# Centring x in place of W1, weights loaded behind the first heads, and attention in thirds of the sequence: a change to a fused attention and MLP kernel on one Trainium2 core

## The chip, the cores and the metric

The kernel runs on one core of one Trainium2 chip. Five engines work side by side, each with its own queue that runs in order: TensorE (PE; its weight loads are shown as PEld), VectorE (DVE), ScalarE (ACT), GpSimd (POOL) and SyncE (SP, which here only issues DMAs). Inputs lie in HBM; data is worked on in SBUF, and matmuls write to PSUM. The metric is device time in microseconds. Three runs of the kernel before took 345.12, 343.38 and 345.32 us (median 345.12).

## The reference

Four batches, 8 heads, 768 positions, head size 64. Each query sees only the 6 chunks (of 32 keys) with the largest upper bound of its score; the result goes through a layer norm and a two-layer MLP.

```python
k_min, k_max = k_chunks.min(3), k_chunks.max(3)          # 24 chunks of 32 keys
ub = sum(maximum(q * k_min, q * k_max), -1)              # bound of each query on each chunk
ub = where(causal, ub, -1e9); top = argsort(ub)[..., -6:]
scores = where(in_top_chunk & (i >= j), q @ k.T / 8, -1e9)
x = softmax(scores) @ v                                   # heads side by side: (4, 768, 512)
xn = (x - mean(x)) / sqrt(var(x) + 1e-6) * g_ln
out = x + maximum(xn @ w_ch1, 0) @ w_ch2                  # 512 -> 2048 -> 512
```

## The kernel before

**Units of work.** A "head" below is a pair of heads `g` of one batch (16 pairs, four to a batch), for two heads fill the 128 partitions (64 values each). A sequence is six blocks of 128 positions. For each `g` the kernel runs these pieces:

- `load_qk` (L183): two DMAs for q and two for k, issued by SP. `load_v` (L193): two DMAs with a cast, issued by POOL, and a memset.
- `prep_q` (L201): six transposes on PE into the PSUM tile `tr`, one ACT copy (`qh`), then on DVE `ql` (L211), `rh` (L214), `rl` (L215) and the copies into `QA` and `QB` (L218, L219).
- `prep_k` (L222): six transposes into `tr`, DVE minimum and maximum over the chunks (L230, L231), two ACT copies (`KA`, `KB`), and small DVE steps that fill `BD`.
- `bounds` (L243, 20 matmuls), `select` (L257, DVE: two additions, ten MAX8, one comparison), `mask_t` (L274, five transposes and two DVE copies). The mask enters the scores as extra rows of `QA` and `QB`.
- `score_bin` (L287): for each head of the pair six bins of scores in PSUM tiles `mm`, each followed by one ACT Exp into `pt`; `diag` (L310, DVE): multiplies the six diagonal blocks by a triangle `Lmask`; `values` (L317): 21 matmuls per head; `normalise` (L331, DVE), once per head of the pair.
- `x_t` (L341): six transposes and one DVE copy give one row of `xT`.

For each batch there are `stats` (L355, DVE, bn_stats over 512 values for each block), `mlp1` (L376, 32 pieces: four matmuls and one ACT Relu each) and `mlp2` (L391, 24 pieces of four matmuls; after each fourth one DVE step `ot` and one output DMA on SP).

**Weights.** POOL loads and casts W1 and W2 in four DMAs each (L147, L152). W1 is multiplied by `g_ln` (`w1_scale`, L155, DVE), its mean over the input features is formed (`w1_mean`, L160, 16 matmuls and four ACT copies) and taken off (`w1_center`, L168, DVE), so that x itself need not be centred.

**Order.** Every piece is given a time by `at(t, fn)` (L410 to L450), where one unit is a head: head `g` has its scores at `g`, its preparation up to two units ahead. The MLP of batch `b` starts at `4(b+1)+0.25`, beside the heads of batch `b+1`; the last MLP has nothing beside it. The pieces are written in order of these times (L453). The framework then orders the instructions by priority and by a model of when their inputs are ready, so an instruction can come ahead of its written place; on the chip each queue runs in the order so fixed.

**Buffers.** `tr` has one buffer of two PSUM banks, `mm` three of one bank, `sm` two, `trh` one. q and k have three buffers, v four.

Of the kernel before, what the change touches and what calls it, by code (L numbers as in the profile page):

```python
# [9 lines left out]
ACTF = mybir.ActivationFunctionType  # L10
# [8 lines left out]
def kernel(  # L19
# [12 lines left out]

    nc = tc.nc
# [6 lines left out]
    NT = S // P  # L40
    HP = H // 2
# [13 lines left out]
    SB0 = S - P  # L55
# [3 lines left out]
    ldp = ctx.enter_context(tc.tile_pool(name="ldp", bufs=3))  # L59
    vap = ctx.enter_context(tc.tile_pool(name="vap", bufs=4))  # L60
    prp = ctx.enter_context(tc.tile_pool(name="prp", bufs=2))
    smp = ctx.enter_context(tc.tile_pool(name="smp", bufs=2))
    ptp = ctx.enter_context(tc.tile_pool(name="ptp", bufs=3))
    xp = ctx.enter_context(tc.tile_pool(name="xp", bufs=2))
    htp = ctx.enter_context(tc.tile_pool(name="htp", bufs=1))
    outp = ctx.enter_context(tc.tile_pool(name="outp", bufs=3))

    PSUM = bass.MemoryType.PSUM
    ps_t = ctx.enter_context(tc.tile_pool(name="ps_t", bufs=1, space=PSUM))
# [4 lines left out]
    q_r = q.rearrange("b h (t p) d -> b p t h d", p=P)  # L74
    k_r = k.rearrange("b h (t p) d -> b p t h d", p=P)
    v_r = v.rearrange("b h (t p) d -> b p t h d", p=P)
    out_r = out.rearrange("b (t p) n -> b t p n", p=P)

    pieces = []

    def at(t, fn):
        pieces.append((t, len(pieces), fn))
# [4 lines left out]
    Lmask = const.tile([P, P], F16, name="Lmask", tag="Lmask")  # L87
    causb = const.tile([P, NT - 1, NCH], F32, name="causb", tag="causb")
    RT = const.tile([P, S], F16, name="RT", tag="RT")
    mean_w = const.tile([P, P], F16, name="mean_w", tag="mean_w")  # L90
    mhalf = const.tile([P, NT], F32, name="mhalf", tag="mhalf")
    NR = 3
    QA = [ring.tile([P, S], F16, name=f"QA{i}", tag=f"QA{i}") for i in range(NR)]
    QB = [ring.tile([P, S], F16, name=f"QB{i}", tag=f"QB{i}") for i in range(NR)]
    KA = [ring.tile([P, S], F16, name=f"KA{i}", tag=f"KA{i}") for i in range(NR)]
    KB = [ring.tile([P, S], F16, name=f"KB{i}", tag=f"KB{i}") for i in range(NR)]

    BD = [ring.tile([P, 2, 2, 2, NCH], F16, name=f"BD{i}", tag=f"BD{i}") for i in range(2)]
    MN = [ring.tile([P, NT - 1, P], F16, name=f"MN{i}", tag=f"MN{i}") for i in range(2)]

    def consts_first():
        make_identity(nc, ident_f)
        nc.vector.tensor_copy(ident_h, ident_f)
        for i in range(2):
            nc.vector.memset(BD[i], 0.0)
        for i in range(2):
            nc.vector.memset(MN[i], 0.0)
        nc.gpsimd.memset(causb, 0.0)
        nc.gpsimd.affine_select(
            out=causb, in_=causb, compare_op=ALU.is_ge, fill=CAUSAL,  # L110
            base=P, pattern=[[P, NT - 1], [-CH, NCH]], channel_multiplier=1,
        )
        nc.gpsimd.memset(RT, 0.0)
        for r0 in (0, 64):
            rr = RT[r0:r0 + NCH, :]
            nc.gpsimd.memset(rr, -NEGM)
            nc.gpsimd.affine_select(
                out=rr, in_=rr, compare_op=ALU.is_ge, fill=0.0,
                base=0, pattern=[[1, S]], channel_multiplier=-CH,
            )  # L120
            nc.gpsimd.affine_select(
                out=rr, in_=rr, compare_op=ALU.is_ge, fill=0.0,
                base=CH - 1, pattern=[[-1, S]], channel_multiplier=CH,
            )
        nc.gpsimd.memset(Lmask, 1.0)
        nc.gpsimd.affine_select(
            out=Lmask, in_=Lmask, compare_op=ALU.is_ge, fill=0.0,
            base=0, pattern=[[1, P]], channel_multiplier=-1,
        )
        nc.gpsimd.memset(mhalf, -0.5)  # L130
        nc.gpsimd.memset(mean_w, 1.0 / DM)

    def consts_ring(i):
        nc.vector.tensor_copy(KA[i][64:P, :], RT[64:P, :])
        nc.vector.tensor_copy(KB[i][0:64, :], RT[0:64, :])
        nc.vector.memset(QA[i][64:P, 0:P], 0.0)
        nc.vector.memset(QB[i][0:64, 0:P], 0.0)
# [5 lines left out]
    w1mean = const.tile([P, HID], F16, name="w1mean", tag="w1mean")  # L143
    w1_r = moe_w_ch1.rearrange("(kt p) n -> p kt n", p=P)
    w2_r = moe_w_ch2.rearrange("(kt p) n -> p kt n", p=P)

    def w1_load(kt):  # L147
        if kt == 0:
            nc.sync.dma_start(gstr, moe_g_ln.rearrange("(kt p) -> p kt", p=P))
        nc.gpsimd.dma_start(w1b[:, kt, :], w1_r[:, kt, :])  # L150
# [3 lines left out]

    def w1_scale(kt):  # L155
        nc.vector.tensor_scalar(
            w1b[:, kt, :], w1b[:, kt, :], gstr[:, kt:kt + 1], None, op0=ALU.mult,
        )

    def w1_mean(j):  # L160
        mp = ps_m.tile([P, 512], F32, name="mm", tag="mm")
        for kt in range(KT1):
            nc.tensor.matmul(
                mp, mean_w, w1b[:, kt, 512 * j:512 * j + 512], start=(kt == 0), stop=(kt == KT1 - 1),
            )
        nc.scalar.copy(w1mean[:, 512 * j:512 * j + 512], mp)

    def w1_center(kt):  # L168
        nc.vector.tensor_tensor(w1b[:, kt, :], w1b[:, kt, :], w1mean, ALU.subtract)  # L169
# [13 lines left out]
    def load_qk(g):  # L183
        b, hp = divmod(g, HP)
        qn = ldp.tile([P, NT, 2, D], F32, name="qn", tag="qn")
        kn = ldp.tile([P, NT, 2, D], F32, name="kn", tag="kn")
        for hh in range(2):
            nc.sync.dma_start(qn[:, :, hh, :], q_r[b, :, :, 2 * hp + hh])
        for hh in range(2):
            nc.sync.dma_start(kn[:, :, hh, :], k_r[b, :, :, 2 * hp + hh])  # L190
        st[g].update(qn=qn, kn=kn)

    def load_v(g):  # L193
        b, hp = divmod(g, HP)
        va = vap.tile([P, 2, NT, 80], F16, name="va", tag="va")
        for hh in range(2):
            nc.gpsimd.dma_start(va[:, hh, :, 0:D], v_r[b, :, :, 2 * hp + hh])  # L197
        nc.gpsimd.memset(va[:, :, :, D:D + 1], 1.0)
        st[g].update(va=va)

    def prep_q(g):  # L201
        qn = st[g]["qn"]
        pst = ps_t.tile([P, S], F32, name="tr", tag="tr")
        for t in range(NT):
            nc.tensor.transpose(pst[:, t * P:(t + 1) * P], qn[:, t, :, :], ident_f)  # L205
        qh = prp.tile([P, S], F16, name="qh", tag="qh")
        ql = prp.tile([P, SB0], F16, name="ql", tag="ql")
        rh = prp.tile([P, SB0], F16, name="rh", tag="rh")
        rl = prp.tile([P, SB0], F16, name="rl", tag="rl")
        nc.scalar.activation(qh, pst, ACTF.Copy, scale=QS)  # L210
        nc.vector.scalar_tensor_tensor(  # L211
            ql, pst[:, P:S], QS, qh[:, P:S], op0=ALU.mult, op1=ALU.subtract,
        )
        nc.vector.tensor_scalar_max(rh, qh[:, P:S], 0.0)  # L214
        nc.vector.scalar_tensor_tensor(  # L215
            rl, qh[:, P:S], 0.0, ql, op0=ALU.is_gt, op1=ALU.mult,
        )
        nc.vector.tensor_copy(QA[g % NR][0:64, :], qh[0:64, :])  # L218
        nc.vector.tensor_copy(QB[g % NR][64:P, :], qh[64:P, :])  # L219
        st[g].update(qh=qh, ql=ql, rh=rh, rl=rl)  # L220
# [264 lines left out]
```

## Time and profile before

| | |
|---|---|
| median of three runs | 345.12 us |
| the profiled execution's own time | 344.2 us |
| its span in the trace | 342.5 us |
| PE, PEld, DVE busy | 294.4, 182.5, 221.3 us |
| ACT, POOL busy | 188.9, 46.8 us |
| granted PE clock, mean | 0.97 |
| DMA moved | 26.63 MB, 78 GB/s over the span |

The profile shows one execution. Its second part cuts the span into 40 slices of 8.56 us; a digit is the busy share of an engine in tenths. The chain (fourth part) is what ended last, followed backwards through whatever released each step. A group's row (fifth part) gives busy time, the mean length of one instruction, and the idle time just before its instructions with what ended it. The ends of matmuls are modelled, and successive instructions overlap in the records, so the price of one instruction in a dense run is the distance from its start to the next start, as the timeline shows it, and not its own length.

### The profile page before, as it was taken

What the parts mean: (1) busy time and instruction counts of PE and PEld (TensorE: products, weight loads), DVE (VectorE), ACT (ScalarE), POOL (GpSimd) and SP (SyncE); (2) the same over time, 40 slices, a digit from 0 to 9 for tenths busy, and PEclk for the clock granted to TensorE, in tenths of its full rate; (3) what the DMA queues carried; (4) which work ended last, traced back from release to release, by engine and by line L of the source; (5) the groups of instructions that cost most, each with busy time, mean ns of one, the idle gap of its engine ahead of it and who ended that gap; (6) DMA issues with size and microseconds to landing.
All of it is one profiled execution on the core that took longest, in us unless ns stands there. A gap on an engine that the chain in (4) does not pass through costs nothing.

```text
span 342.5 us, 6455 instructions
## 1 busy us (share of the span) xinstructions
PE 294.4 (86%) x2528; PEld 182.5 (53%) x2528; DVE 221.3 (65%) x645; ACT 188.9 (55%) x373; POOL 46.8 (14%) x79
## 2 busy tenths in 40 slices
PE   2226678786599999999999999998998999999995
PEld 1214456354366665656666656565665554565442
DVE  4839898999995656878965766869862543710111
ACT  2103686776387865454978764537787635166100
POOL 8940020121112020202030202020100000010000
PEclk9985898999899999999999999999999999999999
DMA  9999998582623432737152442322000011100021
GB/s 177 184 213 183 196 210 137 71 115 49 69 48 24 94 25 80 116 91 130 49 71 48 60 89 44 72 44 43 2 3 0 2 61 61 63 2 0 31 94 61
DMA packets 81966, 26.63 MB, mean 78 GB/s; under 512 B 76304, under 2 KB 78352, under 8 KB 81936
## 3 DMA queue, kind: packets, MB, share of 16 engines
q1 hardware_dynamic: 54160, 18.88, 23.9%
q0 software_dynamic: 27776, 7.34, 21.0%
q8 instruction: 20, 0.33, 0.4%
q14 instruction: 10, 0.08, 0.1%
HBM read 27.27 MB, written 6.29 MB: 98 GB/s over the span
## 4 chain that ended last, share of the span: by engine, by line
PE 63%; DVE 20%; ACT 8%; POOL 4%; DMA 3%; issue 1%; ACTq 0%; POOLq 0%
PE mm L383 22%; PE mm L396 22%; PE mm L297 7%; PE sm L326 3%; DMA w1b<-in_moe_w_ch_dram 3%; PE sm L251 3%; DVE m L268 3%; DVE ql L211 2%; ACT pt L306 2%; DVE rl L215 2%; ACT hT L387 2%; PE tr L205 2%; ACT KB L233 2%; POOL va L197 1%; ACT KA L232 1%; DVE w1b L169 1%
## 5 line engine op out<-in xcount | busy, mean ns | idle before, releaser
L306 ACT ACTIVATE pt<-mm 128x512 f16<-128x512 f32 (+1 forms) x192 | 99.5, 548 | 47.5 <-PE mm L297 46.5
L383 PE MATMUL mm<-xT,w1b 128*128 128x512 f16 (+1 forms) x512 | 98.4, 328 | 5.8 <-DVE xT L350 2.7
L396 PE MATMUL mm<-w2b,hT 128*128 128x512 f16 x384 | 93.1, 379 | 0.5 <-ACT pt L306 0.5
L387 ACT ACTIVATE hT<-mm 128x512 f16<-128x512 f32 (+1 forms) x128 | 59.8, 493 | 37.3 <-PE mm L383 37.1
L383 PEld LDWEIGHTS <-w1b 128*128 128x128 f16 x512 | 48.7, 98 | 37.0 <-issue 6.7
L396 PEld LDWEIGHTS <-hT 128*128 128x128 f16 x384 | 35.1, 97 | 33.1 <-issue 0.8
L197 POOL DMA_DIRECT2D va<-in_v_dram x32 | 27.0, 849 | 153.4 <-issue 125.8
L403 DVE SCALAR_TENSOR_TENSOR ot<-mm,rstd,x_all 128x512 f32<-128x512 f32 x24 | 17.9, 747 | 41.0 <-PE mm L396 41.0
L326 PEld LDWEIGHTS <-pt 128*128 128x128 f16 x672 | 30.4, 98 | 13.4 <-DVE pt L313 3.3
L297 PE MATMUL mm<-QA,KA 128*128 128x512 f16 (+3 forms) x128 | 33.1, 325 | 4.4 <-DVE QA L279 4.3
L313 DVE TENSOR_TENSOR pt<-pt,Lmask 128x768 f16<-128x768 f16 x32 | 17.7, 553 | 29.0 <-ACT pt L306 29.0
L326 PE MATMUL sm<-va,pt 128*128 128x65 f16 x672 | 34.5, 194 | 1.2 <-DVE pt L313 1.0
L297 PE MATMUL mm<-QB,KB 128*128 128x512 f16 (+3 forms) x128 | 32.1, 309 | 2.2 <-ACT pt L306 1.5
L205 PE MATMUL tr<-ident_f,qn 128*128 128x128 f32 x96 | 18.2, 315 | 9.0 <-DMA qn<-in_q_dram 4.8
L232 ACT CAST KA<-tr 64x768 f16<-64x768 f32 x16 | 12.6, 789 | 23.2 <-DVE kx L231 23.2
L226 PE MATMUL tr<-ident_f,kn 128*128 128x128 f32 x96 | 16.9, 292 | 9.0 <-DVE ql L211 9.0
L210 ACT ACTIVATE qh<-tr 128x768 f16<-128x768 f32 x16 | 13.1, 819 | 16.4 <-PE tr L205 16.4
L251 PE MATMUL sm<-BD,qh 128*128 128x96 f16 x80 | 15.2, 215 | 6.3 <-DVE BD L239 6.3
L261 DVE TENSOR_TENSOR ubt<-sm,causb 128x240 f32<-128x240 f32 x16 | 6.5, 407 | 21.2 <-PE sm L251 21.1
L297 PEld LDWEIGHTS <-KA 128*128 128x128 f16 x128 | 12.7, 103 | 13.8 <-DVE QA L279 4.4
L226 PEld LDWEIGHTS tr<-ident_f,kn 128*128 128x128 f32 x96 | 12.4, 151 | 13.1 <-DVE ql L211 10.1
L297 PEld LDWEIGHTS <-KB 128*128 128x128 f16 x128 | 12.4, 99 | 11.9 <-issue 3.5
(67 smaller groups left out, 361.6 us busy)
## 6 DMA issues: line engine op xcount, KB each, us to landing
qn<-in_q_dram SPq DMA_DIRECT2D x32, 192.0 KB, 3.3
kn<-in_k_dram SPq DMA_DIRECT2D x32, 192.0 KB, 4.0
out_dram<-ot SPq DMA_DIRECT2D x24, 256.0 KB, 2.0
va<-in_v_dram POOLq DMA_DIRECT2D x32, 96.0 KB, 3.6
w1b<-in_moe_w_ch_dram POOLq DMA_DIRECT2D x4, 512.0 KB, 11.4
w2b<-in_moe_w_ch_dram POOLq DMA_DIRECT2D x4, 512.0 KB, 21.1
gstr<-in_moe_g_ln_dram SPq DMA_DIRECT2D x1, 2.0 KB, 5.6
```

The source lines that it names most:

```text
L197: nc.gpsimd.dma_start(va[:, hh, :, 0:D], v_r[b, :, :, 2 * hp + hh])
L205: nc.tensor.transpose(pst[:, t * P:(t + 1) * P], qn[:, t, :, :], ident_f)
L226: nc.tensor.transpose(pst[:, t * P:(t + 1) * P], kn[:, t, :, :], ident_f)
L251: nc.tensor.matmul(o, a[:, c0:c0 + P], bd[:, arr].rearrange("p l h c -> p (l h c)"), start=(i == 0), stop=(i == 3),)
L297: nc.tensor.matmul(sc[:, o:o + c1 - c0], ks[:, t * P:(t + 1) * P], qs[:, c0:c1], start=True, stop=True,)
L306: nc.scalar.activation(dst, sc[:, 0:o].rearrange("p (a c) -> p a c", a=len(segs)), ACTF.Exp, scale=SCALE / QS,)
L313: nc.vector.tensor_tensor(dv, dv, Lmask.unsqueeze(1).to_broadcast([P, NT, P]), ALU.mult,)
L326: nc.tensor.matmul(pv[:, s, 0:D + 1], flat[:, c0:c0 + P], va[:, hh, t, 0:D + 1], start=(t == 0), stop=(t == s),)
L383: nc.tensor.matmul(hp_[:, 0:cw], w1b[:, kt, m * P:(m + 1) * P], xT[:, kt, c0:c0 + cw], start=(kt == 0), stop=(kt == KT1 - 1),)
L387: nc.scalar.activation(hts[b][:, m, c0:c0 + cw], hp_[:, 0:cw], ACTF.Relu, scale=HS)
L396: nc.tensor.matmul(yp, hts[b][:, kt, s * P:(s + 1) * P], w2b[:, kt, :], start=(kt == 0), stop=(kt == KT2 - 1),)
L403: nc.vector.scalar_tensor_tensor(ot, yp, rs[b][1][:, s:s + 1], x_all[:, s].rearrange("p h d -> p (h d)"), op0=ALU.mult, op1=ALU.add,)
```

## The change

The pieces and their order change together.

- **The norm.** `w1_scale`, `w1_mean` and `w1_center` go. `stats` runs for each head over its 128 columns; `centre` combines the four and writes x minus its mean in float16 (`xc`), block by block; `x_t` transposes `xc` for the whole batch, and the copy from PSUM to `xT` multiplies by `g_ln`, which now lies on the partitions.
- **Weights.** The loads of W1 and W2 each lie behind a small POOL copy (`w_gate`) from the `kc` tile of head 1 and of head 3. `g_ln` is loaded from ACT's queue.
- **Thirds.** q and k are transposed and prepared in three pieces of 256 positions; `tr` gets two buffers of one bank. Scores, the triangle, values and normalise work on a third (two blocks) of both heads of a pair, diagonal blocks first in `pt`. The triangle becomes a POOL `affine_select` of 128x512; `Lmask` goes.
- **Chunk bounds.** `BD` is filled by four steps over 128 partitions in place of five, four of them on 64.
- **Order and buffers.** A head `g` of the first batch stands at `g-4`, later ones at `g-4+1.5` (`GAP`). The MLP of batch 0 stands from 0.2 on, over 5.5 units. q and k get four buffers, v five, `pt` two for each third, `ot` two; the ring of `QA`, `QB`, `KA`, `KB` and `BD` has five slots.

The counts of DMAs for q, k, v, weights and output stay as they are.

```diff
-    ps_t = ctx.enter_context(tc.tile_pool(name="ps_t", bufs=1, space=PSUM))
+    ps_t = ctx.enter_context(tc.tile_pool(name="ps_t", bufs=2, space=PSUM))
...
+        for i in range(NK):
+            nc.vector.tensor_copy(KA[i][64:P, :], RT[0:64, :])
+            nc.vector.tensor_copy(KB[i][0:64, :], RT[0:64, :])
...
+    def w_gate(w, g):
+        nc.gpsimd.tensor_copy(w[0:1, 0, 0:1], st[g]["kc"][0:1, 0, 0:1])
...
-    def w1_scale(kt):
-    def w1_mean(j):
-    def w1_center(kt):
...
+    def turn(g, nm, t0, t1):
+        pst = ps_t.tile([P, 512], F32, name="tr", tag="tr")
...
+    def prep_q(g, t0, t1):
...
+        nc.scalar.activation(qh[:, c], pst, ACTF.Copy, scale=QS)
...
+        eng.tensor_copy(QA[g % NK][0:64, c], qh[0:64, c])
+        eng.tensor_copy(QB[g % NK][64:P, c], qh[64:P, c])
+    def prep_k(g, t0, t1):
...
+        nc.vector.tensor_reduce(kc[:, 0, n], view, axis=AX.X, op=ALU.min)
+        nc.vector.tensor_reduce(kc[:, 1, n], view, axis=AX.X, op=ALU.max)
+        nc.scalar.copy(KA[g % NK][0:64, c], pst[0:64, :])
+        nc.scalar.copy(KB[g % NK][64:P, c], pst[64:P, :])
+    def prep_b(g):
+        nc.vector.tensor_tensor(kc[:, 1], kc[:, 1], kc[:, 0], ALU.subtract)
+        nc.vector.tensor_tensor(km, kc.unsqueeze(2).to_broadcast([P, 2, 2, NCH]), hsel_b, ALU.mult)
+        nc.vector.tensor_copy(bd[:, :, 0], km)
+        nc.vector.tensor_tensor(bd[:, :, 1], km, bd[:, :, 0], ALU.subtract)
...
+    def score_bins(g, r, hh):
+        segs = [(2 * r + 1, 2 * r + 1, 1), (2 * r, 2 * r, 2)] + [(t, 2 * r, 2) for t in range(2 * r)]
...
+    def diag(g, r):
+        dv = st[g]["pt", r][:, 0:2].rearrange("p n h x -> p (n h) x")
+        nc.gpsimd.affine_select(
+            out=dv, in_=dv, compare_op=ALU.is_ge, fill=0.0,
+            base=0, pattern=[[0, 4], [1, P]], channel_multiplier=-1,
+        )
...
+    def stats(g, t0, t1):
+            nc.vector.bn_stats(rs[b]["st"][:, s, hp, :], x_all[:, s, 2 * hp:2 * hp + 2, :]...)
+    def centre(b, t0, t1):
+            nc.vector.bn_aggr(r["mv"][:, s, :], r["st"][:, s])
+            nc.vector.tensor_scalar(
+                r["xc"][:, s, :], x_all[:, s].rearrange("p h d -> p (h d)"),
+                r["mv"][:, s, 0:1], None, op0=ALU.subtract,
+            )
+    def x_t(b, kt, t0, t1):
...
+        nc.vector.tensor_scalar(
+            xT[:, kt, t0 * P:t1 * P], px[:, 0:(t1 - t0) * P], gstr[:, kt:kt + 1], None, op0=ALU.mult,
+        )
...
+    GAP = 1.5
     for g in range(NG):
+        T = float(g - HP) + (GAP if g >= HP else 0.0)
+        at(T - 2.8 if g > 3 else -8 + 0.1 * g, load_qk, g, 0, NR)
+        at(T - 2.6 if g else T - 3.2, load_v, g, 0, NT)
+        for t0 in (0, 2, 4):
+            at(T - 1.98 + 0.09 * t0, prep_q, g, t0, t0 + 2)
+            at(T - 1.90 + 0.09 * t0, prep_k, g, t0, t0 + 2)
+        at(T - 1.3, prep_b, g)
+        at(T - 0.98, bounds, g, 0, NT)
+        at(T - 0.97, select, g, 0, NT, n_sel)
+        at(T - 0.45, mask_t, g, 0, NT, n_sel)
+        for r in range(NR):
+            at(T + 0.3 * r, score_bins, g, r, 0)
+            at(T + 0.3 * r + 0.1, score_bins, g, r, 1)
+            at(T + 0.3 * r + 0.3, diag, g, r)
+            at(T + 0.3 * r + 0.4, values, g, r)
+            at(T + 0.3 * r + 0.45, normalise, g, r)
+            at(T + 0.3 * r + 0.47, stats, g, 2 * r, 2 * r + 2)
+    at(-4.5, w_gate, w1b, 1)
+    at(-2.9, w_gate, w2b, 3)
     for kt in range(KT1):
+        at(-4.4 + 0.01 * kt, w1_load, kt)
+        at(-2.8 + 0.01 * kt, w2_load, kt)
     for b in range(B):
+        e = 4.0 * b + (GAP if b > 0 else 0.0)
+        for r in range(NR):
+            at(e - 1 + 0.3 * r + 0.475, centre, b, 2 * r, 2 * r + 2)
+        for kt in range(KT1):
+            at(e + 0.10 + 0.01 * kt, x_t, b, kt, 0, NT)
+        at(e + 0.2, rstd, b, 0, NT)
+        e = e + 0.15
+        d = 4.0 * (b + 1) + GAP + 0.15 - e
+        if b == B - 1:
+            d = 4.0
...
```

## The prediction, made before the changed kernel ran

> **What bounds the kernel now.** I read the slices of the page first, then the table by stage, the waits, the chain in order of time and the timeline.
>
> ```profile
> PE   2226678786599999999999999998998999999995
> ...
> DVE  4839898999995656878965766869862543710111
> ```
>
> ```profile
> 30.00:40.00 10.00, 7.97 (x52) 5.40 (x50) 8.19 (x28) 7.57 (x15) 0.00 (x0) 0.67 1.32 188
> ...
> 50.00:60.00 10.00, 7.53 (x95) 5.73 (x93) 8.75 (x25) 6.33 (x13) 0.70 (x1) 0.83 0.91 141
> ...
> 80.00:90.00 10.00, 5.60 (x69) 3.67 (x67) 9.96 (x29) 3.03 (x7) 1.91 (x3) 1.00 0.69 98
> ...
> 110.00:120.00 10.00, 9.42 (x89) 6.40 (x88) 6.67 (x16) 8.82 (x18) 0.00 (x0) 1.00 0.35 80
> ...
> 130.00:140.00 10.00, 10.00 (x107) 6.31 (x105) 5.99 (x22) 4.95 (x9) 0.09 (x1) 1.00 0.24 75
> ```
> Columns: stretch and length, busy PE, PEld, DVE, ACT, POOL, PE clock, DMA share, GB/s. There are two regimes. Up to about 90 us only heads run, and DVE is full (idle gaps between 30 and 90 us add up to 3.4 us) while PE idles. From there PE is full and DVE has slack.
>
> ```profile
> DVE w1b L156 <- DMA w1b<-in_moe_w_ch_dram: 7.0, 2, 5.9
> ```
> In the first regime DVE also stood 7.0 us before `w1_scale`, waiting for W1.
>
> ```profile
> 89.58 0.48 DVE xT L350
> ...
> 90.10 0.39 PE mm L383
> ...
> 296.68 20.92 PE mm L383 x128
> 317.59 20.73 PE mm L396 x96
> ...
> 338.35 0.75 DVE ot L403
> ```
> The chain shows where the regimes meet, 90.1 us, and the last MLP alone: 41.65 us. Four cost 166.6. The tail from 338.35 to the end of the span is 4.15.
>
> The rest of the span, 342.5 - 90.1 - 166.6 - 4.15 = 81.7, is head work and stalls; nine mlp1 matmuls (1.8 us) had run before 90.1, so it is 83.4. PE's price of a head, start to start in the timeline: transposes 12 in 1.36, bounds 0.85, mask 0.28, scores 5376 columns at 0.213 for 512 = 2.24, values 42 at 0.031 = 1.30, x transposes 0.34; sum 6.37. Open at 90.1 were heads 5 to 15 (70.1) and the rest of head 4 (2.8), less prepared work of heads 5 and 6 (3.6): 69.3. So PE lost 14.1 us in stalls after 90.1.
>
> **The change part by part.** The sum has three terms: when the first MLP starts (T0, set by DVE), PE work after it, stalls.
>
> *Norm on W1.* Gone from DVE: four `w1_scale` (0.74), four `w1_center` (1.13), and the 7.0 us wait; 14.5 us, all before 90.1. The 16 matmuls of `w1_mean` (3.4 us of PE) lay in PE's idle time: nothing.
>
> *Order.* Before, DVE had done more than four heads by 90.1: BD, selection and mask of head 4 (3.8), preparation and selection of head 5 (7.0), ql, rh, rl and ring copies of head 6 (2.5), 13.3 us in all. With head 4 and later ones placed 1.5 units on, only the q and k pieces of head 4 precede the MLP.
>
> *DVE per head.* Before, from the timeline between 45.7 and 56 us, start to start: ql 0.74, rh 0.24, rl 0.73, QA and QB 0.75, select 1.81, xT 0.46, two triangles 0.93, reductions 1.85, mask copies 1.04, BD with its subtraction 0.90, two normalises 1.30: 10.75.
> ```profile
> 45.74 0.82 DVE L211 SCALAR_TENSOR_TENSOR ql<-tr,qh 128x640 f16<-128x640 f32 x1 [0.32 <-ACT qh L210]
> 46.48 0.32 DVE L214 TENSOR_SCALAR rh<-qh 128x640 f16<-128x640 f16 x1
> ...
> 51.52 0.95 DVE L230 TENSOR_REDUCE kc<-tr 128x24 f32<-128x768 f32 x1
> 52.39 0.95 DVE L231 TENSOR_REDUCE kx<-tr 128x24 f32<-128x768 f32 x1
> ```
> 640 columns take 0.74 and 768 take 0.87: 0.07 fixed and 1.04 ns a column. After, by that: ql and rl in pieces of 128, 256 and 256: 0.89 each; rh 0.39; six ring copies at 0.23 (a third of 0.36 with 0.16 fixed) 1.38; six reductions of 256 at 0.34: 2.04; BD 0.76; select 1.81 and mask 1.04 as before; three normalises 1.62; six bn_stats of 128 (512 take 0.60) 1.20; triangle and xT leave: 12.0. Lower bound, splitting free: 10.6. Upper, each of 16 extra pieces at the 0.18 of a 64x48 BD step: 13.5. I take 12.0, since the same operation at two lengths fixes it.
>
> [...]
>
> *Constants.* Ten ring copies (some 0.45), ten memsets (0.16) and the rest on DVE end at 9.2 us. `RT` now goes ahead of the identity on POOL; the identity comes at about 4 us, hidden behind q, whose first transpose waited until 4.82. If q came earlier it would cost up to 2.5.
>
> *T0.* 9.2 + four heads 48.1 + q and k of head 4 5.6 + six centrings 2.2 (bn_aggr 0.16, 512 columns 0.2 at the rate of w1_scale's 2048 in 0.74) + four xT 1.8 + gaps 3.4 as before + 3 for the last head's chain Exp, triangle, values, normalise, centre, transposes = 73.3. xT with a scale is between the copy's 0.46 and a one-column-a-cycle 0.87; 0.46 is nearest (same tiles), the other end adds 1.6.
>
> *Triangle on POOL.* Rows: 128x128 0.29, 24x768 0.82; 512 columns between, 0.61; three a head, with v's two DMA issues (1.7) 3.7 us of POOL in some 12: hidden. But POOL disturbs DVE:
> ```profile
> 10.51 0.62 DVE L214 TENSOR_SCALAR rh<-qh 128x640 f16<-128x640 f16 x1
> ...
> 26.06 0.32 DVE L214 TENSOR_SCALAR rh<-qh 128x640 f16<-128x640 f16 x1
> ```
> The first ran while POOL issued v's DMAs, the second while POOL was idle. Nine such fast copies a head, each up to 0.3 longer for 3.7/12 of the time: up to 0.8 a head, 3.3 at T0; least, nothing. I leave it out of the point and keep it for the range. [...]
>
> *ACT.* The Exps keep number and columns (six bins, 2688 columns for each head). qh, KA and KB in 256s cost 0.28 start to start (Exp of 256) times nine, against 0.72 + 1.60: 0.2 more a head, hidden while ACT has its 1.2 us in ten (row 110); uncovered, 2.4 for twelve heads.
>
> *PE.* 24 score matmuls in place of 16, same columns. The last mlp1 ran 128 matmuls, half of them 256 wide, in 20.92 against 20.5 by columns, so weight loads hide: least 0, most 8 x 0.1 a head; I take 0.
>
> *DMA and queues.* Same DMAs. On SP, head 3's loads now find a fourth buffer free; later ones are written 1.2 units after their buffer's last reader, so outputs behind them aren't held. On POOL, W1's gate waits for `kc` of head 1 (about 23 us by the DVE sum); behind it stand v of later heads and the first triangle, wanted only after 25 us. W1 then needs 11.4 us, W2 (gate near 47) 21.1: landed by 68, wanted at mlp2 near 94. Each us of the gate past 25 would delay the first values.
>
> *PE after T0.* Heads 4 to 15, 76.4, less 1.36 done: 75.1. Stalls: 14.1 as before. Two `tr` buffers relieve it, bins in bursts of up to three on three `mm` buffers load it; least 7, most 24. The last batch is new: after the last values come normalise 0.54, two bn_stats 0.4, centring 0.74, and four rounds of transposes and xT on one `trh` buffer 4.0; 1.36 of it is counted and two mlp2 pieces (1.72) cover: 3 with handoffs (0 to 6).
>
> Sum: 73.3 + 166.6 + 75.1 + 14.1 + 3 + 4.15 = 336.3 of span. The profiled execution took 344.2 with 342.5 of span, so 1.7 more: **338 us**. That execution is 0.9 below the median 345.12; I don't correct for it.
>
> **Rivals.**
> - *DVE pieces cost more (slower).* Place: the first four heads. At 14.2 us a head T0 moves by 8.8. Beside MLP 0, DVE's 67 us (heads 4 to 7, preparation of 8 and 9) becomes 78 against PE's 75.8, 2.2 more: 349. It passes the old median from 13.8 us a head. For it: the POOL row, and more handoffs between small pieces. Against: the two reductions.
> - *Bursts of scores.* A third bin fills `mm`; the next mlp1 piece waits for an Exp (0.5). At 0.8 a head for twelve heads: 348; the earlier start is paid back. For it: waits of mm on Exps exist already; against: they are 1.6 us after 90.
> - *More than forecast.* Splitting nearly free (11.2 a head, T0 70), stalls 7, no loss at the last batch: 325. For it: double `tr`; against: more handoffs.
> - *The start moves but work doesn't shrink.* Part of the forecast already: of 16.8 us at T0, 5.8 is head work left for later (75.1 against 69.3).
>
> **How the numbers follow.** Forecast 0.50 (332 to 344), more 0.17, bursts 0.15, DVE 0.18. The range 324 to 350 takes in the ends of all and leaves out some 2 in 10. About 1% is what a measurement of this kernel can tell from no change. Faster by over 1% (below 341.7): 0.17 and 0.45 of the forecast's, 0.62. Within 1%: 0.05 of the forecast's, bursts, 0.20. Slower: 0.18.
>
> **What would show it.** Right: the first dense mlp1 near 73 us, no wait of DVE for W1, 12.0 us of DVE a head before it, PE in nines from there, PE idle of about 3 us before the last mlp1. Wrong: T0 past 80, `rh` and ring copies at twice their length beside POOL, or PE waiting for Exps after each burst.

## The result and the profile after

The changed kernel takes 359.05 us (median of four runs, 358.35 to 359.70) against 344.28 us for the kernel before beside it: ratio 1.0427, 95% interval 1.038 to 1.0475. It is 14.8 us slower, and 9 us above the upper end of the range. The profiled execution took 358.35 us, its span is 356.6.

The slices of the page, kernel after (8.9 us each):

```profile
PE   1547378759999899977999989989999999799995
...
DVE  8996669996797798998568677989474545500021
```

PE reaches its nines a little sooner than before, and that is the early start the change was to bring. But two new things show. At the fifth digit (36 to 45 us) PE falls to 3 while DVE is at 6, so neither engine is full there. And where PE held nine after nine before, there are now sevens: slices 18 and 19 (152 to 169 us) and 35 (303 to 312 us), at the ends of batches 1 and 3.

The table by stage, kernel after (stretch, length, busy PE, PEld, DVE, ACT, POOL, PE clock, DMA share, GB/s):

```profile
40.00:50.00 10.00, 7.51 (x87) 6.12 (x84) 3.98 (x24) 5.67 (x15) 3.97 (x7) 0.64 1.55 205
...
130.00:140.00 10.00, 9.71 (x88) 5.98 (x89) 8.62 (x30) 7.01 (x17) 1.39 (x2) 1.00 0.48 124
...
160.00:170.00 10.00, 7.27 (x50) 5.22 (x51) 9.00 (x37) 4.18 (x12) 1.36 (x1) 0.83 0.24 66
```

In the first regime DVE works 7.7 to 9.5 of 10 us in each row, except from 40 to 50 us, where it works 3.98. In the second regime DVE has less slack than before (8.62 against 5.99 from 130 to 140 us), and at 160 us, the end of batch 1, PE falls to 7.27.

The chain in order of time, kernel after, says what the hole at 40 us is and where the regimes meet:

```profile
26.60 16.40 DMA kn<-in_k_dram
...
84.73 0.38 PE mm L404 x2
...
331.73 20.73 PE mm L420 x96
```

The k of head 3 landed at 43.0 us (26.60 + 16.40), and the chain of what set the end goes through that transfer. The first matmuls of mlp1 run at 80 us, and from 84.73 they run dense (before: 90.1). So the start is 5.4 us sooner, but what follows takes 271.9 us (356.6 - 84.73) where it took 252.4. The last MLP itself is no slower: its mlp2 takes 20.73 us in both.

The waits, kernel after (engine, tile and line, what it waited for: us, times, longest):

```profile
PE tr L193 <- DMA kn<-in_k_dram: 5.5, 3, 2.2
PE trh L387 <- DVE xc L368: 4.1, 5, 1.6
PE trh L387 <- DVE xT L390: 4.0, 6, 1.3
```

No wait of DVE for `w1b` is left. But PE now waits in `x_t` (L387), for the centring (`xc`) and for its own one buffer (until the copy `xT` has emptied it). PE's timeline at the end of batch 1, kernel after:

```profile
157.83 0.22 PE L387 MATMUL trh<-ident_h,xc 128*128 128x128 f16 x1
159.21 0.23 PE L387 MATMUL trh<-ident_h,xc 128*128 128x128 f16 x1 [1.16 <-DVE xc L368]
...
161.40 0.23 PE L387 MATMUL trh<-ident_h,xc 128*128 128x128 f16 x1 [1.55 <-DVE xc L368]
162.91 0.49 PE L387 MATMUL trh<-ident_h,xc 128*128 128x128 f16 x6 [1.27 <-DVE xT L390]
```

A transpose of a block of `xc` stands at the head of PE's queue until DVE, full with the next head's work, has centred that block; nothing else of PE's appears in these gaps. Two such stops (1.16 and 1.55 us) and one for the buffer (1.27) take 4.0 us here. PE's clock was 0.83 in the row from 160 us.

### The profile page after: what moved, and what is told of

The parts are those of the page before. It is cut to its first block, busy times and chain, and to the rows that moved or that the text cites. A ratio compares the mean times of both kernels' runs of the same rounds, so it can differ in the third digit from the quotient of the medians.

```text
span 356.6 us, 7179 instructions
## 1 busy us (share of the span) xinstructions
PE 303.0 (85%) x2640; PEld 197.0 (55%) x2640; DVE 243.3 (68%) x952; ACT 196.7 (55%) x465; POOL 75.1 (21%) x122
## 4 chain that ended last, share of the span: by engine, by line
PE 53%; DVE 21%; ACT 10%; SPq 7%; DMA 5%; issue 2%; POOL 0%; ACTq 0%
PE mm L404 19%; PE mm L420 16%; SPq L172 7%; PE mm L301 6%; DMA kn<-in_k_dram 5%; ACT pt L306 4%; PE sm L328 3%; PE tr L193 3%; ACT hT L408 3%; PE sm L248 3%; DVE m L268 2%; DVE x_all L339 2%; DVE xT L390 2%; DVE ql L206 2%; DVE bst L359 2%
## 5 line engine op out<-in xcount | busy, mean ns | idle before, releaser
L306 ACT ACTIVATE pt<-mm 128x384 f16<-128x384 f32 (+1 forms) x192 | 95.1, 552 | 47.4 <-PE mm L301 36.2
L314 POOL TENSOR_SCALAR_AFFINE_SELECT pt<-pt 128x512 f16<-128x512 f16 x48 | 31.6, 659 | 168.2 <-ACT pt L306 168.2
L427 DVE SCALAR_TENSOR_TENSOR ot<-mm,rstd,x_all 128x512 f32<-128x512 f32 x24 | 17.9, 744 | 40.7 <-PE mm L420 40.5
L301 PE MATMUL mm<-QA,KA 128*128 128x256 f16 (+1 forms) x192 | 32.3, 271 | 5.1 <-ACT pt L306 1.6
L193 PE MATMUL tr<-ident_f,kn 128*128 128x128 f32 x96 | 22.6, 318 | 16.2 <-DVE ql L206 9.8
L301 PE MATMUL mm<-QB,KB 128*128 128x256 f16 (+1 forms) x192 | 33.2, 266 | 2.4 <-ACT pt L306 0.8
L205 ACT ACTIVATE qh<-tr 128x256 f16<-128x256 f32 x48 | 18.8, 391 | 28.0 <-PE tr L193 28.0
L338 DVE RECIPROCAL rden<-sm 128x4 f32<-128x4 f32 x48 | 8.6, 179 | 35.3 <-PE sm L328 35.0
L193 PE MATMUL tr<-ident_f,qn 128*128 128x128 f32 x96 | 22.6, 315 | 11.1 <-DMA qn<-in_q_dram 8.9
L227 ACT CAST KA<-tr 64x256 f16<-64x256 f32 x48 | 17.4, 363 | 20.8 <-DVE kc L226 20.6
L301 PEld LDWEIGHTS <-KB 128*128 128x128 f16 x192 | 17.7, 101 | 12.3 <-issue 4.8
L359 DVE BATCH_NORM_STATS2 bst<-x_all 128x6 f32<-128x128 f16 x96 | 23.9, 284 | 0.8
```

The costliest lines, as they stand in the source:

```text
L193: nc.tensor.transpose(pst[:, (t - t0) * P:(t - t0 + 1) * P], src[:, t, :, :], ident_f)
L205: nc.scalar.activation(qh[:, c], pst, ACTF.Copy, scale=QS)
L301: nc.tensor.matmul(sc[:, o:o + w * P], ks[:, t * P:(t + 1) * P], qs[:, s * P:(s + w) * P], start=True, stop=True,)
L306: nc.scalar.activation(pt[:, done:done + o // P, hh, :], sc[:, 0:o].rearrange("p (n x) -> p n x", x=P), ACTF.Exp, scale=SCALE / QS,)
L314: nc.gpsimd.affine_select(out=dv, in_=dv, compare_op=ALU.is_ge, fill=0.0, base=0, pattern=[[0, 4], [1, P]], channel_multiplier=-1,)
L359: nc.vector.bn_stats(rs[b]["st"][:, s, hp, :], x_all[:, s, 2 * hp:2 * hp + 2, :].rearrange("p h d -> p (h d)"),)
```

## The experiments

My theory after this reading: **H**, the batch ends (centring on DVE, then `x_t` of the whole batch on one buffer) cost PE most. Its rivals: **T**, late transfers, because the gates leak; **D**, preparation in thirds costs DVE and PE more than it gives; **P**, the triangle on GpSimd. Times are medians; the ratio is to the kernel before, run beside it on the same chip (its median was 343.8 to 345.0 each time). Differences in the text are of medians; taken from the ratios they shift by up to 1.3 us. e2, e7 and e9 leave out the mean, e8 the mean and `g_ln`: they price a part of the change and cannot replace it.

| run | from | us | ratio, 95% interval |
|---|---|---|---|
| e1_gate_all | after | 353.12 | 1.0222 (1.018 to 1.0264) |
| e2_xt_head | after | 348.29 | 1.0081 (1.0046 to 1.0117) |
| e3_prep_whole | after | 349.94 | 1.0125 (1.0065 to 1.0186) |
| e4_diag_dve | after | 359.44 | 1.0423 (1.0351 to 1.0494) |
| e5_gate_prep | after | 351.33 | 1.0187 (1.013 to 1.0244) |
| e6_gate_prep_xtsplit | after | 347.55 | 1.01 (1.0069 to 1.0131) |
| e7_gate_prep_xthead | after | 335.35 | 0.9739 (0.969 to 0.9787) |
| e8_before_nonorm | before | 332.84 | 0.9662 (0.9597 to 0.9728) |
| e9_xthead_centred | after | 339.36 | 0.9827 (0.9767 to 0.9887) |
| e10_before_scale_act | before | 342.64 | 0.9935 (0.9906 to 0.9964) |
| e11_before_thirds | before | 344.68 | 1.0007 (0.9981 to 1.0033) |
| e12_before_xc | before | 367.39 | 1.0662 (1.0603 to 1.072) |
| e13_norm_early_pool | before | 353.15 | 1.0278 (1.0229 to 1.0328) |
| e14_norm_early_dve | before | 343.15 | 0.9964 (0.9934 to 0.9993) |
| e15_xt_two_buffers | after | 346.37 | 1.0055 (1.0023 to 1.0087) |
| e16_prep_two_split | after | 346.50 | 1.0059 (1.003 to 1.0087) |
| e17_gate_prep_two_split | after | 347.42 | 1.0086 (1.0059 to 1.0114) |

### One part undone: e1 to e4

**e1, the gates.** `w_gate` writes one element of slice 0. The loads of the other slices don't depend on it and were ordered ahead of it. POOL's timeline, kernel after:

```profile
9.64 1.63 POOL L149 DMA_DIRECT2D w1b<-in_moe_w_ch_dram  x3
...
13.26 0.77 POOL L152 DMA_DIRECT2D w2b<-in_moe_w_ch_dram  x1
17.34 0.18 POOL L143 CAST w1b<-kc 1x1 f16<-1x1 f32 x1 [3.31 <-DVE kc L225]
```

Three of four loads of W1 and one of W2 precede the first gate.

```
-        nc.gpsimd.tensor_copy(w[0:1, 0, 0:1], st[g]["kc"][0:1, 0, 0:1])
+        step = w.shape[1] // 4
+        nc.gpsimd.tensor_copy(
+            w[0:1, 0:w.shape[1]:step, 0:1], st[g]["kc"][0:1, 0, 0:4].unsqueeze(2),
+        )
```

> The one-element copy that holds the weights back is made to write one element of every slice that a load fills (four of W1, four of W2), where after.py writes slice 0 alone. Transfers theory: three of four loads of each weight ran from 9.6 us on, beside the q and k loads of heads 1 to 3, and SyncE stood at its issues until 26.6 us and kn of head 3 landed at 43; with all loads behind the gates the k of head 3 lands by 35, the first MLP starts 6 to 10 us sooner, and the time is 349 to 353. Stall theory (the lost time lies in the heads and batch ends after the first MLP starts): the first MLP may start sooner, but DVE is what then sets its start (four heads of 12 us after about 11 us), so that at most 3 us come back: 356 to 360. If both weights now land later than the first MLP needs them, PE shows a wait for w1b or w2b and the time does not fall.

353.12, 5.9 us less. Here the four W1 loads are issued behind the gate, the k of head 3 lands at 35.2 us, and the hole is gone; the table by stage of e1:

```profile
40.00:50.00 10.00, 5.78 (x74) 4.08 (x72) 9.81 (x41) 6.03 (x16) 4.73 (x7) 0.93 1.30 196
```

DVE works 9.81 of 10 where it worked 3.98, and the first mlp1 matmul moves from 80.05 to 75.84 us. T is real and worth 5.9 us, just short of the range it had promised; most of the 15 is elsewhere.

**e2, x^T head by head.** `centre` keeps `bn_aggr` and loses its subtraction; `x_t` takes a head.

```
-        for kt in range(KT1):
-            at(e + 0.10 + 0.01 * kt, x_t, b, kt, 0, NT)
+        at(T + 1.12, x_t, g)
...
-                px[:, (s - t0) * P:(s - t0 + 1) * P], rs[b]["xc"][:, s, kt * P:(kt + 1) * P], ident_h,
+                px[:, s * P:(s + 1) * P],
+                x_all[:, s, 2 * hp:2 * hp + 2, :].rearrange("p h d -> p (h d)"), ident_h,
```

> Leaves out: the mean is not taken off x (no centred copy, no wait for the whole batch); x^T of a head is made from x_all right behind that head's last third, with g in the copy, as a step of each head in place of four steps behind the batch. Batch-end theory: the four transposes and copies of a batch run in a ping-pong on one PSUM buffer behind the centring, 10 to 12 us in three batch ends that PE loses, and the six centring copies (2.2 us of DVE a batch) go too; the time falls to 345 to 350 and the batch stretches from 82 and 80 us to about 77. Transfers theory: the first MLP starts only 2 to 3 us sooner and the rest as before, 355 to 357. Small-pieces theory: DVE is what is late in the middle of the batches, so only the DVE time saved (about 2.5 us a batch) comes back: 350 to 354.

348.29, 10.8 us less: within H's range. The first mlp1 matmul comes at 70.7 us where it came at 80.05, so much of the gain lies at the first batch's end.

**e3, preparation whole.**

```
-        for t0 in (0, 2, 4):
-            at(T - 1.98 + 0.09 * t0, prep_q, g, t0, t0 + 2)
-            at(T - 1.90 + 0.09 * t0, prep_k, g, t0, t0 + 2)
+        at(T - 1.98, prep_q, g, 0, NT)
+        at(T - 1.60, prep_k, g, 0, NT)
```

with one `tr` buffer of 768 columns, and W2's gate 0.35 later.

> q and k of a head are turned and split whole (one PSUM buffer of 768 columns in place of two of 256), as before the change: per head 7 DVE instructions fewer by half (14 instead of 42 in the preparation), and two round trips of PE and DVE in place of six. Small-pieces theory: DVE a head falls from about 13 to 11 us, and PE is stopped at two preparations a head and not six, so that 10 to 15 us come back: 344 to 350. Batch-end theory: at most 3 us. Transfers theory: a whole head must have landed before its first transpose, so nothing or a loss: 357 to 362.

349.94, 9.1 us less. DVE's work falls from 243.3 to 223.2 us, 1.26 us a head, and the first mlp1 comes at 68.3 us (in the profiled execution, the fastest of the four at 347.13). D is real as well, in this kernel.

**e4, the triangle back on DVE.**

```
-        nc.gpsimd.affine_select(
-            out=dv, in_=dv, compare_op=ALU.is_ge, fill=0.0,
-            base=0, pattern=[[0, 4], [1, P]], channel_multiplier=-1,
-        )
+        nc.vector.tensor_tensor(dv, dv, Lmask.unsqueeze(1).to_broadcast([P, 4, P]), ALU.mult)
```

> The triangle of the diagonal blocks is multiplied on DVE again (one tensor_tensor of 512 columns a third, 36 more of about 0.4 us in 12 of the 16 heads' places, 48 in all) and GpSimd keeps its loads and memsets alone. GpSimd theory (its 659 ns select stands in the chain from the Exp to the values, and slows DVE's fast copies beside it): the time falls by 4 to 10 us, MN goes back from 0.7 to 0.35 us. Small-pieces theory (DVE is nearly full): 48 times 0.4 us more on DVE, 2 to 12 us slower: 361 to 371. Transfers theory: within 2 us of after.

359.44, no difference. The 48 multiplications take 20.0 us of DVE. Other DVE work gets some 6 us shorter without POOL beside it (the `QA` copies 210 ns for 269, `MN` 397 for 450). P falls: the triangle costs about the same on either engine. The equal time is made of two shifts, though: in the profiled executions dense mlp1 starts at 88.42 us, 3.7 later than in the changed kernel, and what follows is 3.9 us shorter. PE had run much the same work by then (490 matmuls, and 486).

### Together: e5 to e9

```
e5  the edits of e1 and e3
e6  e5 and:
-            at(e + 0.10 + 0.01 * kt, x_t, b, kt, 0, NT)
+            at(e - 0.20 + 0.01 * kt, x_t, b, kt, 0, 4)
+            at(e + 0.10 + 0.01 * kt, x_t, b, kt, 4, NT)
e7  the edits of e1, e2 and e3
e8  the kernel before and:
-        at(1.55 + 0.3 * kt, lambda kt=kt: w1_scale(kt))
-        at(2.75 + 0.2 * kt, lambda kt=kt: w1_mean(kt))
-        at(3.50 + 0.2 * kt, lambda kt=kt: w1_center(kt))
e9  e7, with the subtraction of centre kept; nothing reads xc
```

e5:

> The weights gated in every slice (worth 5.9 us alone) and q and k prepared whole (worth 9.1 us alone) together; the reference's computation is whole. If the two losses are independent, 359.1 - 5.9 - 9.1 = 344, level with the kernel before. If both are one and the same late start (the transfers of heads 2 and 3 and the preparation of the same heads lie beside each other), the larger alone is left: 349 to 350.

e6:

> As the gated and whole one, and x^T of a batch is made in two goes: tokens 0 to 511 ahead of the last third's values, tokens 512 to 767 behind its centring; four copies more a batch on DVE (about 0.3 us each), the computation is whole. Batch-end theory: what PE waits for behind the last centring is cut to four rounds of two transposes, and the first goes lie under the Exps of the last third: 3 to 7 us less than the gated and whole one, 337 to 341. If DVE's load is what counts (1.2 us more a batch), nothing or 1 to 3 us more: 344 to 347.

e7:

> Leaves out: the mean is not taken off x. Gated, prepared whole, and x^T made head by head from x_all with g in the copy. If the three losses (5.9, 9.1 and 10.8 us) are independent, 359.1 - 25.8 = 333; if all three shorten the same late first MLP and share it, 338 to 342. It bounds from below what a version of this change can reach with these orders.

e8:

> The kernel before with the twelve steps on W1 taken out (scale by g, column mean, centring); leaves out g and the mean. It is what the change could win at most by taking them off DVE ahead of the first MLP, with nothing in their place. Theory of the prediction: 14.5 us of DVE before 90 us are on the path that sets the first MLP, so 12 to 15 us faster, 330 to 333. Rival: DVE's work there was partly cover for other waits (loads of heads 2 and 3), and only the 4.3 us of PE's column means and the wait for W1's scale come off: 336 to 341.

e9:

> The gated, whole-prepared kernel with x^T head by head (335.4 us), and the 24 centring copies are made all the same, for nobody: they load DVE where they did, and nothing waits for them. Leaves out: x^T is not centred. The 12 to 16 us between it and the kernels that transpose the centred copy (351.3, and 347.6 in two goes) are split so. Waiting theory: what costs is that no transpose can start before the batch is centred, and this runs at 335 to 338. Load theory: the 8.1 us of copies themselves hold up DVE at the batch ends, and it runs at 341 to 344.

- e5, 351.33: not the sum. With the whole preparation, tighter gates gain nothing (349.94 without them). T and D together give 7.7 us, not 15; I read it that both shorten the same late start.
- e6, 347.55: 3.8 us below e5. The absolute times that I had expected assumed that e5 would reach 344.
- e7, 335.35: 16.0 us below e5. This is the batch end, and the largest term of all. About half of it lies at the first batch's end: in the profiled executions dense mlp1 starts at 78.43 us in e5 and at 71.07 in e7.
- e8, 332.84: taking the norm off W1 is worth 11.0 us, with nothing in its place. The first mlp1 matmul comes at 73.2 us instead of 81.3.
- e9, 339.36: the copies themselves cost 4.0 us. The other 12.0 of the 16.0 are not their load; the waits of e5 show 6.2 us of PE for the centring and 4.9 for the buffer, 11.1 together, and e9 has neither. Both theories missed by a little; the wait is about three times the load.

e7 has the other parts of the change, without the thirds of q and k and without the centring, and is 2.5 us slower than e8: score order, triangle on POOL, statistics by head, later weights and the new times gain nothing on balance.

Along this chain of runs the 15.2 us from the kernel before (343.8 beside e8) to the changed kernel split into -11.0 (norm), +2.5 (rest), +16.0 (batch ends) and +7.7 (start: e5 to after). Each step is a difference of two neighbours in the chain, so that they add up proves nothing; another order of the steps could give other shares.

### One part alone in the kernel before: e11 and e12

```
e11
-        at(g - 1.98, lambda g=g: prep_q(g))
-        at(g - 1.60, lambda g=g: prep_k(g))
+        for t0 in (0, 2, 4):
+            at(g - 1.98 + 0.09 * t0, lambda g=g, t0=t0: prep_q(g, t0, t0 + 2))
+            at(g - 1.90 + 0.09 * t0, lambda g=g, t0=t0: prep_k(g, t0, t0 + 2))
e12  e8 with stats, centre, rstd and x_t of the change, and:
-        at(g + 1.17, lambda g=g: x_t(g))
+        at(g + 1.09, lambda g=g: stats(g, 0, NT))
+        at(e - 0.10, lambda b=b: centre(b, 0, NT))
+        for kt in range(KT1):
+            at(e + 0.01 * kt, lambda b=b, kt=kt: x_t(b, kt, 0, NT))
```

e11:

> The kernel before, with one part of the change alone: q and k turned and split in thirds of 256 columns through two PSUM buffers; all else as it was and the computation is whole. Small-pieces theory: what the whole preparation gave back in the changed kernel is lost here, 6 to 11 us slower: 350 to 355. If thirds only cost where the weights' loads and the batch-end steps crowd the start, within 3 us of before: 343 to 347.

e12:

> The kernel before, with the core of the change alone: no scale, mean or centring of W1; x centred on DVE at the batch end with statistics head by head, g in the x^T copy, x^T of the batch behind the centring, and the next batch's first scores ahead of it in the order; the computation is whole. My theory: W1's part gives 11 us as the run without it showed, and the batch ends cost as much or more, so 343 to 350. The prediction's theory (2.2 us of centring and 3 us a batch end): 345 - 11 + 7 = 338 to 341, faster than before.

e11, 344.68: thirds cost nothing here, which D alone did not explain. The table by stage suggests why. First the kernel before, then e11:

```profile
10.00:20.00 10.00, 3.07 (x26) 2.66 (x25) 5.65 (x13) 2.40 (x3) 8.80 (x17) 1.00 1.69 189
20.00:30.00 10.00, 1.86 (x10) 1.47 (x11) 7.04 (x22) 0.00 (x0) 1.80 (x3) 0.64 1.11 201
```

```profile
10.00:20.00 10.00, 4.38 (x29) 3.16 (x30) 9.59 (x32) 3.07 (x9) 8.25 (x16) 1.00 1.70 184
20.00:30.00 10.00, 6.23 (x35) 4.33 (x33) 9.32 (x40) 4.90 (x12) 2.20 (x3) 1.00 1.10 204
```

DVE is busy for 18.91 us of these 20 and not 12.69, where it had waited for W1; no wait of DVE for W1 is left in e11. So, as I read it, the thirds' extra work took the place of the wait. The changed kernel has no such wait to fill, and there the same work lies on the path. No run tests this reading by itself.

e12, 367.39, is the core of the change by itself and the worst kernel here: 34.6 us above e8, far over what I expected. The waits of e12:

```profile
PE trh L383 <- DVE xc L364: 15.4, 8, 5.2
```

PE waits 15.4 us for the centring alone, and 4.2 for the buffer. By the profiles' sums, PE idles 58.5 us of the span in e12 and 39.1 in e8: 19.4 more, which these two waits (19.6) account for. The other 15.8 us of the spans' difference (35.2) are busy time: the same 2512 matmuls take 307.6 us in e12 and 291.8 in e8. The mean granted clock was 0.934 and 0.982; 291.8 times the ratio of the two is 306.8, an estimate that would account for nearly all of it. The clock is low in the rows of the batch ends (0.66 from 80 us and from 240 us, 0.55 from 160 us); the table by stage of e12:

```profile
160.00:170.00 10.00, 6.31 (x33) 3.72 (x34) 8.40 (x31) 2.24 (x4) 1.35 (x1) 0.55 0.21 58
```

In e8 it is 1.00 in every row from 80 to 320 us. So the stops of PE went with a lower clock and longer matmuls; no run here separates the two. The change gives the batch end more room (the centring by thirds of the last head, the next batch's heads 1.5 units on); beside e7 the same step cost 16.0, not 34.6.

### Mending: e10 and e13 to e17

e10, e13 and e14 leave the norm on W1 and take it off the crowded stretch; e15 to e17 mend the batch end.

```
e10  nc.scalar.activation(w1b[:, kt, :], w1b[:, kt, :], ACTF.Copy, scale=gstr[:, kt:kt + 1])
     scale at 2.30 + 0.1 kt
e14  e10, scale at 1.95 + 0.1 kt, means at 2.40 + 0.1 kt, centring at 2.75 + 0.2 kt
e13  e14, the centring by nc.gpsimd.tensor_tensor
e15  e5, x_t: px = ps_s.tile([P, S], F16, name="sm", tag="sm")
e16  e3 with e15's px and e6's two goes;  e17 the same with e1's gates
```

e10:

> The kernel before, with W1's scale by g on ScalarE (an activation with a scale for each partition) and placed later, at 2.30 to 2.60 in the order in place of 1.55 to 2.45; the computation is whole. DVE loses 3.0 us of work and the 7.0 us it waited for w1b to land, ScalarE gets about 7 us. If DVE sets the start of the first MLP, 5 to 9 us faster than before: 335 to 339. If the 7.0 us wait was cover for the loads of heads 2 and 3, only the 3.0 us come back: 341 to 342. If ScalarE is late with the Exps for it, 345 or more.

e13:

> The kernel before, whole computation, W1's normalisation kept but taken out of the late stretch: scale on ScalarE at 1.95 to 2.25 in the order, column means at 2.4 to 2.7, centring on GpSimd at 2.75 to 3.35. The run with the scale on ScalarE gave 342.6; the normalisation in all is worth 11.0 us. If DVE's 4.8 us of centring and PE's 4.3 us of means weigh where they stood (62 to 90 us) and GpSimd has the room (it stood idle from 49 to 59 and from 61 to 71 us), 4 to 8 us less than that run: 335 to 339. If GpSimd's work at 2048 columns (by its 659 ns for 512 columns, some 2.6 us each) slows DVE beside it or comes too late for the first MLP, 342 to 346.

e14:

> As the one with the centring on GpSimd, but the centring stays on DVE, at the same early place. If it is DVE's load and not the place that counts, 0 to 2 us below the run with the scale on ScalarE: 340.5 to 342.6, and above the GpSimd version by 2 to 5 us. If the place counts (the means ahead of 60 us fall into PE's idle time), 337 to 340.

e15:

> The changed kernel gated in every slice and prepared whole (351.3 us, ratio 1.0187), and the batch's x^T transposes go into the two-buffer PSUM pool of the bounds and values in place of the one buffer; whole computation. The wait for the centred batch stays, the ping-pong of transposes and copies on one buffer goes. Ping-pong theory: the 4.9 us that PE waited for the x^T copies come back, 346 to 347.5. Centring theory: the 6.2 us wait for the centring copies is what counts and the ping-pong lies under DVE's copies anyway, 349.5 to 352.

e16:

> The changed kernel with its late start and its batch ends mended as far as the runs showed how, whole computation: q and k prepared whole, x^T through the two-buffer PSUM pool, and in two goes (tokens 0 to 511 ahead of the last third's values). Weights held back in slice 0 alone, as in the change. From the runs: whole preparation 349.9; the two buffers took 5.0 us off (351.3 to 346.4); the two goes 3.8 us (351.3 to 347.6), but that gain lay partly in the same wait for the one buffer. If the two add up, 341 to 342.5; if they overlap, 344 to 346, level with the kernel before. Under 340 would say that the wait for the centring is gone too, which I do not expect.

e17:

> The same with every slice of the weights held back. Whole preparation with all slices held back ran at 351.3 against 349.9 without, so the holding back is worth nothing or costs 1 us where the preparation is whole: 342 to 346, within 1.5 us of its twin. A gain of 4 us or more would say that the transfers were still what was late.

**e10**, 342.64, lies 0.65% below the kernel before, and its interval with it: the fastest kernel here that computes everything, by less than the 1% of the forecast. The gain of 2.4 us is about the 3.0 us of scaling; the 7.0 us of waiting did not come back. The waits of e10:

```profile
DVE ql L209 <- ACT qh L208: 11.6, 6, 5.0
```

This wait was 6.1 us in the kernel before. The timelines of ACT and DVE in e10 show where it comes from:

```profile
22.17 2.00 ACT L156 ACTIVATE w1b<-w1b,gstr 128x2048 f16<-128x2048 f16 x1 [5.77 <-DMA w1b<-in_moe_w_ch_dram]
24.19 0.81 ACT L208 ACTIVATE qh<-tr 128x768 f16<-128x768 f32 x1
...
25.03 0.82 DVE L209 SCALAR_TENSOR_TENSOR ql<-tr,qh 128x640 f16<-128x640 f32 x1 [5.02 <-ACT qh L208]
```

It is the same wait for W1 in another queue: the scale stands at the head of ACT's queue until W1 has landed, the `qh` of the next head stands behind it, and DVE waits for that `qh`. So e10 does not test what the 7.0 us are worth. **e14**, 343.15, no better: moving the norm earlier as well gains nothing, and its scale waits in ACT's queue in the same way (6.11 us). A scale ordered behind the landing of W1 was not run. **e13**, 353.15, lost 10 us to the centring on POOL (see the last section).

**e15**, 346.37, 5.0 us below e5 (4.5 by the ratios): a second buffer is worth about what PE had waited for the one. The waits of e5, then of e15:

```profile
PE trh L390 <- DVE xc L371: 6.2, 4, 2.8
...
PE trh L390 <- DVE xT L393: 4.9, 8, 1.3
```

```profile
PE sm L390 <- DVE xc L371: 5.2, 3, 2.1
...
PE sm L390 <- DVE x_all L342: 2.1, 2, 2.0
PE sm L390 <- DVE xT L393: 1.9, 4, 0.7
```

The wait for the buffer falls from 4.9 to 1.9 us, but a new one of 2.1 (for the normalised x) stands beside it, so the waits at these transposes fall by 1.9 us in all; the rest of the gain is not in these rows.

**e16**, 346.50: the two mends overlap, for the two goes add nothing to the second buffer. 11 us above e7 are left; 4.0 of them are the copies (e9), and PE still waits 8.4 us for the centring. **e17**, 347.42: the gates gain nothing. So no version with x centred that I ran beats the kernel before.

## Why the prediction was wrong, step by step

- **The step that failed** is the price of the handoff from centring to transposes. The sum has it as "3 for the last head's chain Exp, triangle, values, normalise, centre, transposes" in T0 and "The last batch is new ... 3 with handoffs (0 to 6)" in "PE after T0"; for the batch ends between, "Stalls: 14.1 as before". There I counted DVE's instructions and no wait, because PE had other work; but that work stood behind the waiting transpose in PE's queue. Against e7 the batch ends cost 16.0 us: 4.0 of copies, and 12.0 that the waits of e5 (11.1) nearly account for. About half of it lies at the first batch's end, in T0. By the predicted 75.1 us of head work, the stalls after 84.73 come to 356.6 - 84.73 - 4.1 - 164.5 (the MLPs, less 2.1 us already run) - 75.1 = 28.2 and not 17.1.
- **"DMA and queues" failed too.** "W1's gate waits for `kc` of head 1 ... landed by 68", costed at nothing. The gate held one slice in four. The early loads delayed k of head 3 to 43.0 us; e1 puts that at 5.9 us. The element that the gate writes, in the diff, shows it.
- **T0**, 73.3 forecast, 84.73 measured for dense mlp1, 11.4 late. The DVE work in it was right in size: 66.9 by the terms of the sum, 66.26 busy in the first 80 us (some of head 4's later steps are among it, and three of the four `xT` are not). The 0.87 that the forecast has as the other end for `xT` with a scale is what a reduction of 768 columns takes before, start to start; `xT` takes 0.61 us on the mean, and the plain copy before took 0.55. The idle time was 13.7 where I had 6.4, and 6.0 of it lie in the row from 40 to 50 us, the late k. The rest is the first batch's own end: from 80 to 84.73 us, mlp1 pieces alternate with rounds of transposes. The span is 20.3 us over the forecast 336.3: 11.4 in T0 and the rest in the stalls, which I have only as what is left over.
- **DVE per head** held: 12.0 forecast; 243.3 less 50.3 for outputs, `xT`, centring and constants, over 16, is 12.06; the lengths taken off overlap their neighbours, so some 0.3 more is possible (an estimate). The estimate from two lengths held for the pieces too: start to start, a reduction of 256 columns takes 0.34 us and a ring copy 0.23 (timeline of the kernel after, from 51.28 us), both as forecast. The rival on it (from 13.8) is refuted; no run shows its 14.2 us a head. Still, the preparation whole gave back 9.1 us, where 1.26 a head on four heads is 5.0.
- **Norm on W1**: 14.5 forecast for T0, 11.0 by e8, where the first mlp1 comes 8.1 us sooner. Wrong in size. Which part is short is open: e10 keeps the wait in another queue, and e11, which has lost it, has the thirds' work in its place.
- **Triangle on POOL**, taken off DVE and costed at nothing on POOL: right for T0, where e4 starts 3.7 us later, as four heads at 0.93 would have it; after T0 e4 gains 3.9 us, so the triangle on POOL has a price there that the sum left out. What it consists of stays open. **Scores in bursts**: not seen; PE's waits of score matmuls for Exps are 2.4 us in all.
- **"More than forecast"** took double `tr` for a gain; e11 and e3 show none.

Not settled: where the other 4 us of e3's gain lie. The first loads of the weights run as early there, but the k of head 3 is issued at 25.4 us and lands at 40.7, just before PE takes it at 40.85; in the changed kernel it landed at 43.0. Why SP issued it sooner I did not find out. The 2.5 us between e7 and e8 are open too.

## What to carry to other kernels

When work moves from a constant (W1, once) to the data (x, each batch), cost it at every place where its result crosses to another engine, with everything queued in order behind the waiting instruction; busy time alone hides it, and here about 11 of 16 us were the wait. An instruction that waits takes its wait along to the queue it is moved to (e10: 5.77 us on ACT, and 5.02 us of DVE behind it): ask what stands behind it there. And a dependency set by hand holds only what it writes (three of four loads of W1 ran ahead of the gate; one that holds every slice gave 5.9 us, e1): follow each load it is to hold back.

## What the runs showed of the chip

Beside a POOL `tensor_tensor` (two SBUF inputs, 4156 ns on the mean) four DVE instructions took 3.44 to 5.37 us each, where the same ones take 0.35 to 0.82 without it. POOL's timeline in e13, where W1's four centrings of 128x2048 ran (I had expected 2.6 us each), then DVE's:

```profile
66.24 12.48 POOL L167 TENSOR_TENSOR w1b<-w1b,w1mean 128x2048 f16<-128x2048 f16 x3 [6.71 <-ACT w1mean L164]
...
80.40 4.07 POOL L167 TENSOR_TENSOR w1b<-w1b,w1mean 128x2048 f16<-128x2048 f16 x1
```

```profile
66.48 4.23 DVE L311 TENSOR_TENSOR pt<-pt,Lmask 128x768 f16<-128x768 f16 x1 [0.45 <-ACT pt L304]
70.63 0.81 DVE L209 SCALAR_TENSOR_TENSOR ql<-tr,qh 128x640 f16<-128x640 f32 x1
71.36 3.44 DVE L212 TENSOR_SCALAR rh<-qh 128x640 f16<-128x640 f16 x1
74.73 4.67 DVE L213 SCALAR_TENSOR_TENSOR rl<-qh,ql 128x640 f16<-128x640 f16 x1
79.32 5.37 DVE L216 COPY QA<-qh 64x768 f16<-64x768 f16 x1
```

`pt`, `rh`, `rl` and `QA` take 0.55, 0.35, 0.82 and 0.36 us on the mean in e14, where the centring is on DVE. Each ends within 0.7 us after the end of a `tensor_tensor` on POOL; `QA` stood beside v's two DMA issues (from 78.67 us) and the fourth one. `ql`, with one input in PSUM, runs at its usual 0.82. The four are 15.6 us longer together; less the 4.8 us of centring that DVE no longer does, that is 10.8, about the 10 us that e13 lost to e14. PE shows no wait for the centred W1. Why these four took longer and `ql` did not, the rows do not say: `pt` and `rl` have two SBUF inputs, `rh` and `QA` have one, and so has `ql` beside its input in PSUM. The affine selects of the change (one input, 659 ns) cost less: with them the `QA` copies take 269 ns on the mean, and 210 in e4, which has none; `rh` takes 236 and 213.
